# Output weights loaded two rows per partition and reordered on chip, w_down seven rows per partition, new order tables

## The chip, the cores and the metric

The kernel runs on one core of a Trainium2 chip, which has eight. The core has five engines that run side by side, each with its own instruction stream: TensorE (PE; its weight loads are shown as PEld), VectorE (DVE), ScalarE (ACT), GpSimd (POOL) and SyncE (SP), which here issues every DMA. Sixteen DMA engines move data between the chip's memory (HBM) and the on-chip memory (SBUF). TensorE writes its results to a second on-chip memory, PSUM. The metric is the device time of one launch in microseconds (us); smaller is better.

## The reference

One decode step for four sequences through two layers. Each layer is an attention block and a gated feed-forward block, both with a residual; both layers use the same weights and the same caches.

```python
# attention: B=4, D=512, 32 query heads in 8 groups of 4, Sk=4096, Dh=128
q = layernorm(x) @ wq                     # wq [512, 4096]
p = softmax(q @ k_cache.T * 128**-0.5)    # per head, over 4096 keys
x = x + (p @ v_cache) @ wo                # wo [4096, 512]
# feed-forward: F=1792
h = sigmoid(n @ w_gate) * (n @ w_up)      # n = layernorm(x)
x = x + h @ w_down                        # w_down [1792, 512]
```

The caches are bf16: for every sequence b (0 to 3) and every key/value group u (0 to 7) there is one K block and one V block of 4096 x 128, 1.049 MB each (1024 KB). That makes 64 blocks, all of them needed in both layers.

## The kernel before

**Units and steps.** A unit is one (layer, b, u); there are 64. Two units with neighbouring u form a pair, and the main loop runs over 33 steps: step g computes the scores and the softmax of pair g and the values (P times V) of pair g-1. `ORDER` fixes which pair each step has; the two layers are interleaved. In this text K8 or V8 is the block of unit 8, which is the first unit of pair 4.

**Slots.** K and V blocks land in 12 slots of 1 MB. The four megabytes of wq become four more slots when wq has been used for the last time (`wq_done`). A table `RET` says which blocks stay in their slot from layer 0 to layer 1 and are not loaded again: 31 of 128. So the DMA stream is 97 block loads plus wq, wo, w_gate, w_up and w_down, 115.6 MB.

**The stream.** All loads stand in one list, written as strings in `LOADS` (k: next K block, v: next V block, o: next eighth of wo, s: next half of w_gate, w_up or w_down). `pump()` issues from the head of that list on SP as long as a slot is free, and stops at the first block that finds none. Slots come free in program order: after `scores` of a unit (its K slot) and after `pv` of a unit (its V slot), unless the block stays. SP issues in order, so one load that waits for a slot holds up everything behind it.

**A step.** On PE: `scores` (32 matmuls for a pair, two groups of 16, the first of which may be issued early, at the place `FIRST_AT[g]` of the step before), `spread_max`, `pv` of the previous pair (two groups of 32), `ptrans` (two transposes of the exponentials), `sums`, and now and then a `wo` pair (32 matmuls). On DVE: `k_turn` (the 32x32 transpose of a K block, whole or in two halves), the maximum, and small work. On ACT: the exponential and the 16 copies that put `ptrans` in place, of which `SHARE[g]` groups of four go to DVE. `STEP[g]` codes three choices: modulo 3, where the first `k_turn` stands; the next bit, whether the first `pv` stands ahead of `spread_max`; the last bit, whether the second `k_turn` is cut in halves around the softmax. A place inside a step is numbered 0 to 8.

**Passes.** When the last pair of a sequence's layer-0 attention is done, 23 small stages carry x through the output product, the layer norm, w_gate and w_up (`wide`, 56 matmuls each), the gate, w_down (`down`, 56 matmuls), the second layer norm and the new queries. They are serial, and `PLACES[b]` lays them out over the places of about two steps; (1, 8) is place 8 of the step that closes the sequence, (2, 0) place 0 of the next. The four passes begin at 83.0, 142.3, 196.5 and 253.8 us of the span, for sequences 0, 1, 2 and 3. After the last step a tail does the same for all four sequences at once, in layer 1.

**Layouts that the change touches.** `wparts` gives the source and the destination of every weight load. Before, an eighth of wo (four heads, 512 rows) is loaded with row p of head h in partition p, so each piece in memory is one row, 1 KB. The two halves of w_down hold two consecutive rows per partition, 2 KB pieces; therefore `wide_mm` picks w_gate and w_up columns with a step of 2, so that the result falls into the order in which w_down lies.

Of the kernel before, what the change touches and what calls it, by code (L numbers as in the profile page):

```python
# [55 lines left out]

PLACES = [
    (
        (2, 1), (2, 2), (2, 2), (2, 2), (2, 2), (2, 2),
        (2, 2), (2, 2), (2, 3), (2, 3), (2, 3), (2, 3),  # L60
        (2, 3), (2, 3), (2, 3), (2, 3), (2, 5), (2, 8),
        (3, 1), (3, 5), (3, 5), (3, 6), (3, 6),
    ),
    (
        (1, 8), (2, 0), (2, 0), (2, 0), (2, 0), (2, 2),
        (2, 2), (2, 2), (2, 2), (2, 4), (2, 5), (2, 5),
        (2, 7), (3, 1), (3, 1), (3, 1), (3, 2), (3, 2),
        (3, 2), (3, 5), (3, 5), (3, 6), (3, 6),
    ),
    (  # L70
        (1, 8), (1, 8), (1, 8), (1, 8), (1, 8), (1, 8),
        (1, 8), (2, 0), (2, 2), (2, 3), (2, 3), (2, 4),
        (2, 5), (2, 8), (2, 8), (3, 0), (3, 0), (3, 0),
        (3, 0), (3, 1), (3, 2), (3, 5), (3, 5),
    ),
    (
        (1, 8), (1, 8), (1, 8), (1, 8), (1, 8), (1, 8),
        (1, 8), (2, 0), (2, 2), (2, 3), (2, 3), (2, 4),
        (2, 5), (2, 7), (2, 8), (3, 0), (3, 0), (3, 0),
        (3, 0), (3, 1), (3, 2), (3, 5), (3, 5),  # L80
    ),
]


FIRST_AT = (
    1, 2, 8, 2, 2, 1, 8, 2,
    7, 2, 4, 3, 3, 4, 8, 8,
    1, 8, 4, 2, 2, 2, 8, 2,
    5, 1, 2, 7, 2, 2, 2,
)  # L90

LOADS = (
    "oosk", "vvkok", "", "vkkkvvok", "okokkv", "vskkovoksssskkvvkvvvkkvk", "", "",
    "kkvvkkvvk", "", "", "vvkkvv", "", "kvkk", "", "",
    "vkvkvkvkvkkkk", "vvvvvkkvvk", "vk", "", "kvkkvvkvkvvkvkvkkv", "", "", "",
    "", "vvkkvkvkv", "vkk", "", "", "vvkkv", "", "kkvkvvv",
    "kvvkkvvvv",
)


SHARE = (
    0, 0, 0, 2, 0, 1, 0, 0,
    0, 0, 1, 0, 0, 1, 0, 0,
    1, 0, 0, 1, 0, 0, 0, 2,
    1, 0, 1, 2, 1, 0, 1,
)


WO_AT = (
    3, 2, 1, 0, 2, 1, 3, 2,  # L110
    0, 3, 2, 0, 0, 3, 2, 1,
    0, 2, 0, 0, 1, 0, 1, 2,
    1, 2, 1, 2, 0, 0, 0, 0,
)


# [5 lines left out]
)  # L122


STEP = (
    9, 7, 10, 1, 0, 0, 7, 1,
    1, 6, 6, 7, 9, 8, 0, 6,
    6, 3, 6, 6, 6, 6, 6, 6,
    9, 6, 6, 7, 1, 6, 6, 6,
    7,  # L130
)


# [101 lines left out]
def bass_interleave_layers__gqa_block_cached__glu_gated_glu__decode_kernel(  # L235
# [17 lines left out]
    P = 128  # L253
# [128 lines left out]
    for kinds in LOADS:  # L382
        for kind in kinds:
            if kind == "o":
                loads.append(("wo", got["o"]))
            elif kind == "s":
                loads.append(w_small.pop(0))
                continue
            else:
                need(kind, got[kind])  # L390
            got[kind] += 1
# [3 lines left out]

    KH = KF // 2
    wparts = {
        "wo": lambda n: (wo_sb[:, n * REP:(n + 1) * REP, :],
                         A_wo[n * REP * P:(n + 1) * REP * P, :].rearrange("(h p) n -> p h n", p=P)),
        "wg": lambda n: (wg_sb[:, 2 * n:2 * n + 2, :].rearrange("p i f -> p (i f)"),  # L400
                         B_w_gate[2 * n * P:(2 * n + 2) * P, :].rearrange("(p i) f -> p (i f)", i=2)),
        "wu": lambda n: (wu_sb[:, 2 * n:2 * n + 2, :].rearrange("p i f -> p (i f)"),
                         B_w_up[2 * n * P:(2 * n + 2) * P, :].rearrange("(p i) f -> p (i f)", i=2)),
        "wd": lambda n: (wd_sb[:, 8 * n:min(KF, 8 * n + 8), :].rearrange("p (j i) n -> p j (i n)", i=2),
                         B_w_down[8 * n * P:min(KF, 8 * n + 8) * P, :].rearrange("(j p i) n -> p j (i n)", p=P, i=2)),
    }
    assert KF == 2 * KH
    wkeys = {"wg": ["wg0", "wg1"], "wu": ["wu0", "wu1"], "wd": ["wd0", "wd1"]}
# [52 lines left out]
    def dve(fn, reads=(), writes=()):  # L461
        return S.inst("dve", fn, reads=reads, writes=writes)
# [52 lines left out]
    for p in range(2):  # L515
        dve((lambda p: lambda e: e.memset(qz_sb[p][:, :, :], 0.0))(p), writes=[f"qz{p}"])
    dve(lambda e: e.memset(M_ps[1][:, :], 0.0), writes=["M1"])

    def head_masks():
        dve(  # L520
            lambda e: e.tensor_reduce(half_f, ident_bf.rearrange("p (s w) -> p w s", s=4), AX.X, ALU.add),
            reads=IDENT,
            writes=QC,
        )
        dve(
            lambda e: e.tensor_reduce(
                head_s.rearrange("p (u h) -> p u h", u=2),
                half_f.rearrange("p (u a h) -> p u h a", u=2, h=REP),
                AX.X,
                ALU.add,  # L530
            ),
            writes=QC,
        )
        dve(lambda e: e.tensor_copy(head_b[:, :], head_s), reads=QC, writes=["head"])
        for u in range(2):
            dve(
                (lambda u: lambda e: e.tensor_copy(
                    mask_f[:, :, u, :, :],
                    head_b[:, u * REP:(u + 1) * REP].unsqueeze(1).unsqueeze(1).broadcast_to([P, 4, 4, REP]),
                ))(u),  # L540
                reads=["head"],
                writes=[f"mask{u}"],
            )
        dve(
            lambda e: e.tensor_reduce(half_f, ident_bf.rearrange("p (n h) -> p n h", h=REP), AX.X, ALU.add),
            reads=IDENT,
            writes=QC,
        )
        dve(
            lambda e: e.tensor_reduce(  # L550
                strip_f.rearrange("p (s a) -> p s a", s=4),
                half_f.rearrange("p (s u a) -> p s a u", s=4, u=2),
                AX.X,
                ALU.add,
            ),
            writes=QC,
        )
        dve(lambda e: e.tensor_copy(strip_b[:, :], strip_f), reads=QC, writes=["strip"])
        dve(lambda e: e.memset(rowk_f, -exp_scale), writes=["rowk"])
        dve(lambda e: e.memset(zero_f, 0.0), writes=["rowk"])  # L560
        dve(
            lambda e: e.tensor_reduce(blk_f, ident_bf.rearrange("p (a c) -> p a c", a=4), AX.X, ALU.add),
            reads=IDENT,
            writes=["blk"],
        )
# [176 lines left out]
    def wide_mm(nb, which, f0, f1, M, mk):  # L742
        wsb, keys = ((wg_sb, wkeys["wg"]), (wu_sb, wkeys["wu"]))[which]
        fns = []
        for fc in range(f0, f1):
            for k in range(KD):
                fns.append(
                    (lambda fc, k: lambda e: e.matmul(  # L748
                        M[:, 64 + fc * nb:64 + (fc + 1) * nb],
                        lhsT=wsb[:, k, bass.ds(2 * P * (fc // 2) + fc % 2, P, step=2)],  # L750
                        rhs=xc_bf[:, k, 0:nb],
                        start=(k == 0),
                        stop=(k == KD - 1),
                    ))(fc, k)
                )
        S.group("pe", fns, reads=["xcb"] + keys, writes=[mk])
# [388 lines left out]
    def oplace(l, b):  # L1145
        o = owner.get((l, b), (l, b))
        return {(0, 0): 0, (0, 1): 1, (0, 2): 0, (0, 3): 1, (1, 3): 0}[o], 1 if (l, b) in partner else 0
# [16 lines left out]

    def wo_mm(g, p):
        l, b, u = seq[2 * g]
        n, _ = oplace(l, b)
        pb = partner[l, b][1] if (l, b) in partner else None
        nb = 1 if pb is None else 2
        for c, lb in enumerate([(l, b)] if pb is None else [partner[l, b], (l, b)]):  # L1170
            assert held.pop((n, u, c)) == lb
        fns = []
        for c in range(KD):
            for r in range(2 * REP):
                fns.append(
                    (lambda c, r: lambda e: e.matmul(  # L1176
                        O_ps[p][:, 64 + 2 * c:64 + 2 * c + nb],
                        lhsT=wo_sb[:, u * REP + r, bass.ds(2 * P * (c // 2) + c % 2, P, step=2)],
                        rhs=oT_sb[n][:, u * REP + r, 0:nb],
                        start=(r == 0),  # L1180
                        stop=(r == 2 * REP - 1),
                    ))(c, r)
                )
        S.group(
            "pe", fns, reads=[f"oT{n}_{u}_{c}" for c in range(nb)] + [f"wo{u}", f"wo{u + 1}"], writes=[f"O{p}"]
        )

    def wo_add(g, p):
# [18 lines left out]
    ln_a(0, Bn)  # L1207
    ln_b(Bn)
    head_masks()
    k_turn(0)  # L1210
    pump()
    k_turn(1)
    pump()
    q_mm(Bn, 0, HQ)
    q_spread(0, Bn)
    q_blocks(0)

# [29 lines left out]
    assert all(a[1] < b[0] for a, b in zip(spans, spans[1:])), spans  # L1247

    def do_steps(g, w):
        for st in steps.pop((g, w), ()):  # L1250
            st()
        new = g + 1 < NP and fresh.get(seq[2 * g + 2][:2]) == g
        if new and w == PLACES[seq[2 * g + 2][1]][-1][1]:
            q_blocks(g + 1)
        if g + 1 < NP and w == (8 if new else FIRST_AT[g]):
            scores(g + 1, 0)
            pump()
# [134 lines left out]
                close(sg, k)  # L1392
        do_steps(k, 8)
    assert not waiting
    assert not steps
    assert not loads and len(free) == NSLOT + KD

    def x_rows():
# [115 lines left out]
```

## Time and profile before

| what | value |
|---|---|
| median of 3 runs | 314.08 us (311.87 to 314.35) |
| the profiled execution | 313.99 us; its span in the profile is 312.2 us |
| HBM read | 115.61 MB, 370 GB/s over the span |
| DMA busy share of the span (main queue) | 92.5% |
| PE / DVE / ACT / POOL busy | 69% / 59% / 39% / 8% |
| transfers of wo, 8 of 512 KB | 13.5 us from issue to landing (median) |
| transfers of w_down | 1024 KB and 768 KB |
| last V piece landed | 298.4 us |
| last DVE instruction before the store | 309.68 us |

How to read it: the program's first instruction is at 0. Besides the totals, the profile cuts the span into 40 slices of 7.8 us and gives, for each slice, the busy tenths of every engine, the busy share of the 16 DMA engines and the GB/s that they moved. A second view gives the same sums for any window. The timeline lists the instructions of an engine in order, equal ones merged, with the idle time ahead of them and what ended it in brackets. A transfer's landing time is its issue time plus the time from issue to landing in the view of its source line.

### The profile page before, as it was taken

Reading aid. Unit: us, or ns where it says so; the run is one execution under the profiler, and the core shown is the slowest. Engines: PE = TensorE matmul, PEld = TensorE weight load, DVE = VectorE, ACT = ScalarE, POOL = GpSimd, SP = SyncE. Lnnn points to the kernel's source line nnn. Section 1 sums busy time; section 2 is a strip of 40 time slices with the busy share of each in tenths; the row PEclk is TensorE's granted clock in tenths of the full one; section 3 lists DMA queues with packets and bytes.
Section 4 is the critical chain, followed back from the end, with each engine's and each line's share of the span. In section 5 each row is a group of like instructions: output and inputs, shape, how many; then the busy total and the mean of one; then the engine's idle time right before and its main releaser. Section 6 shows DMA issues by size and latency. Waiting matters only on the chain. (4 is left out here: it accounts for less than half of the span.)

```text
span 312.2 us, 12077 instructions
## 1 busy us (share of the span) xinstructions
PE 215.0 (69%) x5204; PEld 157.6 (50%) x5204; DVE 185.2 (59%) x528; ACT 120.3 (39%) x521; POOL 25.9 (8%) x106
## 2 busy tenths in 40 slices
PE   1320447453578876869997958899776668888896
PEld 0310226232365554648665745675555466365686
DVE  4413585575435348485645979674994657358623
ACT  0000254430410576544445645434762351446610
POOL 0000000000000100110010011001011000020200
PEclk9999999999999995555555555555565555565555
DMA  7999999999997999999999999999999976999900
GB/s 291 400 419 408 421 412 394 417 416 399 408 401 302 420 423 421 414 418 400 362 366 407 422 420 408 407 355 411 418 420 418 419 326 225 359 379 421 367 16 3
DMA packets 21217, 116.39 MB, mean 373 GB/s; under 512 B 1960, under 2 KB 6060, under 8 KB 8492
## 3 DMA queue, kind: packets, MB, share of 16 engines
q1 hardware_dynamic: 21164, 115.62, 92.5%
q8 instruction: 41, 0.67, 0.9%
q14 instruction: 12, 0.10, 0.1%
HBM read 115.61 MB, written 0.00 MB: 370 GB/s over the span
## 5 line engine op out<-in xcount | busy, mean ns | idle before, releaser
L1081 ACT ACTIVATE pT<-PT 32x64 bf16<-32x64 f32 x436 | 93.9, 215 | 63.9 <-PE PT L1056 53.9
L925 DVE STREAM_TRANSPOSE slot<-slot 128x1024 f32<-128x1024 f32 (+1 forms) x57 | 98.4, 1730 | 25.9 <-DMA slot<-in_A_k_cache_dram 25.8
L940 PE MATMUL S_ps<-slot,qz 128*32 128x256 bf16 x976 | 61.6, 408 | 23.2 <-DVE slot L925 13.3
L1098 PE MATMUL O_ps<-pT,slot 128*128 128x4 bf16 x1952 | 60.6, 166 | 16.4 <-DMA slot<-in_A_v_cache_dram 10.0
L1098 PEld LDWEIGHTS O_ps<-pT,slot 128*128 128x128 bf16 x1952 | 56.7, 104 | 21.5 <-DMA slot<-in_A_v_cache_dram 10.1
L940 PEld LDWEIGHTS S_ps<-slot,qz 128*32 128x32 bf16 x976 | 28.6, 127 | 38.1 <-DVE slot L925 14.3
L1011 ACT ACTIVATE pe<-S_ps,small 128x256 bf16<-128x256 f32 x32 | 15.5, 485 | 66.2 <-DVE small L999 34.8
L1025 POOL TENSOR_TENSOR small<-small 128x1 f32<-128x1 f32 x64 | 12.4, 194 | 232.8 <-ACT pe L1011 230.3
L1176 PE MATMUL O_ps<-oT,wo 128*128 128x2 bf16 (+1 forms) x640 | 20.0, 165 | 3.7 <-issue 3.2
L1158 DVE TENSOR_TENSOR oT<-O_ps,rden 128x8 bf16<-128x8 f32 x32 | 5.2, 164 | 29.1 <-PE O_ps L1098 26.2
L1176 PEld LDWEIGHTS O_ps<-oT,wo 128*128 128x128 bf16 x640 | 18.8, 104 | 4.8 <-issue 3.2
L963 DVE TENSOR_REDUCE small<-S_ps 128x1 f32<-128x256 f32 x32 | 13.2, 411 | 11.8 <-PE S_ps L940 11.6
L1056 PE MATMUL PT<-ident_bf,pe 128*128 128x128 bf16 x64 | 11.9, 288 | 7.2 <-ACT pe L1011 7.1
L818 PE MATMUL M_ps<-wq,xc_bf 128*1 128x512 bf16 x128 | 15.7, 608 | 0.3
L732 POOL TENSOR_TENSOR qz<-qc,small 128x128 bf16<-128x128 bf16 x32 | 12.6, 401 | 39.2 <-ACT qc L718 39.2
L1075 DVE CAST pT<-PT 32x64 bf16<-32x64 f32 x60 | 13.2, 220 | 2.8 <-PE PT L1056 0.7
L718 ACT ACT_TABLE_LOAD x1 | 1.3, 1283 | 32.6 <-PE M_ps L707 32.6
L707 PE MATMUL M_ps<-qT,ident_bf 128*32 128x32 bf16 (+1 forms) x80 | 1.8, 213 | 15.9 <-DVE qT L689 14.7
L986 PEld LDWEIGHTS MS<-row_max,mask_f 128*128 128x128 bf16 x64 | 4.1, 107 | 15.7 <-DVE row_max L969 12.7
L986 PE MATMUL MS<-row_max,mask_f 128*128 128x16 bf16 x64 | 6.9, 182 | 7.0 <-DVE row_max L969 6.9
L999 DVE CUSTOM_DVE_ANT_0 junk<-MS,small 128x16 bf16<-128x16 f32 x32 | 6.8, 213 | 7.8 <-PE MS L986 7.4
L1034 PEld LDWEIGHTS MS<-head_b,small 128*128 128x128 bf16 x96 | 5.0, 107 | 12.4 <-issue 11.1
(94 smaller groups left out, 190.1 us busy)
## 6 DMA issues: line engine op xcount, KB each, us to landing
slot<-in_A_v_cache_dram SPq DMA_DIRECT2D x49, 1024.0 KB, 10.7
slot<-in_A_k_cache_dram SPq DMA_DIRECT2D x42, 1024.0 KB, 11.5
wq<-in_A_wq_dram SPq DMA_DIRECT2D x4, 1024.0 KB, 8.0
wo<-in_A_wo_dram SPq DMA_DIRECT2D x8, 512.0 KB, 13.5
wq<-in_A_k_cache_dram SPq DMA_DIRECT2D x3, 1024.0 KB, 12.0
slot<-in_A_v_cache_dram SPq DMA_DIRECT2D x8, 256.0 KB, 17.4
wg<-in_B_w_gate_dram SPq DMA_DIRECT2D x2, 896.0 KB, 15.8
wu<-in_B_w_up_dram SPq DMA_DIRECT2D x2, 896.0 KB, 13.6
```

The costliest lines, as they stand in the source:

```text
L732: lambda e: e.tensor_tensor(qz_sb[z][:, :, 0:4 * REP].rearrange("p i (a r) -> p i a r", r=REP), qc_sb[:, b, u:u + 2, :, :].rearrange("p u ...
L818: (lambda k, st: lambda e: e.matmul(M_ps[h][32 * st:32 * st + 1, :], lhsT=xc_bf[:, k, 0:1], rhs=wv[:, k, h, :, st, :], start=(k == 0), sto ...
L925: dve(lambda e: e.transpose(kf, kf), writes=[f"s{st}"])
L940: (lambda t, b2, e_, w0, s: lambda e: e.matmul(S_ps[p][32 * s:32 * s + 8 * REP, 0:2 * P], lhsT=qzf[:, w0:w0 + 8 * REP], rhs=ktv[:, :, s, : ...
L963: lambda e: e.tensor_reduce(m, S_ps[p][:, 0:2 * P], AX.X, ALU.max),
L1011: lambda e: e.activation(to, frm, ACTF.Exp, bias=nm_sb[p], scale=exp_scale, accum_out=sm_sb[p][0],),
L1025: (lambda n: lambda e: e.tensor_tensor(sm_sb[p][n + 1], sm_sb[p][n], top(sm_sb[p][n]), ALU.subtract))(n),
L1056: (lambda j: lambda e: e.matmul(PT[:, j * P:(j + 1) * P], lhsT=pe_sb[p][:, j, :], rhs=ident_bf[:, :], start=True, stop=True))(j)
L1075: (lambda dst, frm: lambda e: e.tensor_copy(dst, frm))(dst, frm),
L1081: (lambda dst, frm: lambda e: e.activation(dst, frm, ACTF.Copy))(dst, frm),
L1098: (lambda x, c, j: lambda e: e.matmul(O_ps[p][:, ul * REP:(ul + 1) * REP], lhsT=vv[:, x * JG + c * 2 + j, :], rhs=pT[:, x, j, 2 * c + ul, ...
L1176: (lambda c, r: lambda e: e.matmul(O_ps[p][:, 64 + 2 * c:64 + 2 * c + nb], lhsT=wo_sb[:, u * REP + r, bass.ds(2 * P * (c // 2) + c % 2, P, ...
```

## The change

Three things.

1. **wo.** Each eighth of wo is loaded with two consecutive rows per partition (2 KB pieces). Rows 2p and 2p+1 of a 256-row block then sit in partition p, which is not the order that the head-wise product wants. TensorE therefore reorders it: `wo_spread` builds two 0/1 matrices of 128 x 128 in `row_sb`, and `wo_turn(m, ...)` takes one block of 256 rows (m = 0 to 15): for each half of the 64 partitions two matmuls of 64 rows x 512 columns into a PSUM bank, then one ACT copy and one DVE copy of 128 x 512 back over the block. `WO_TURN` gives the place of each turn: four ahead of the first step, twelve between place 0 of step 0 and place 1 of step 4.
2. **w_down.** Each half is 7 consecutive rows per partition (7 KB pieces, two equal loads of 896 KB). `wide_mm` therefore takes its weight columns with a step of 7 instead of 2.
3. **Tables.** `PLACES`, `FIRST_AT`, `LOADS`, `SHARE`, `WO_AT` and `STEP` are all new; `ORDER` and `RET` are not. `WO_ORDER` loads the eighths of wo as 2, 3, 0, 1, 4 to 7, all of them among the first 13 weight and block loads after wq. At the start, the query product `q_mm` is issued before the first two `k_turn` instead of after them.

```diff
 PLACES: of sequence 1, the second tuple, and of sequence 3, the last
-        (1, 8), (2, 0), (2, 0), (2, 0), (2, 0), (2, 2),
-        (2, 2), (2, 2), (2, 2), (2, 4), (2, 5), (2, 5),
-        (2, 7), (3, 1), (3, 1), (3, 1), (3, 2), (3, 2),
-        (3, 2), (3, 5), (3, 5), (3, 6), (3, 6),
+        (1, 8), (2, 0), (2, 0), (2, 1), (2, 1), (2, 1),
+        (2, 2), (2, 2), (2, 2), (2, 5), (2, 5), (2, 5),
+        (2, 6), (3, 0), (3, 1), (3, 1), (3, 1), (3, 1),
         (3, 2), (3, 5), (3, 5), (3, 6), (3, 6),
...
-        (1, 8), (1, 8), (1, 8), (1, 8), (1, 8), (1, 8),
-        (1, 8), (2, 0), (2, 2), (2, 3), (2, 3), (2, 4),
-        (2, 5), (2, 7), (2, 8), (3, 0), (3, 0), (3, 0),
-        (3, 0), (3, 1), (3, 2), (3, 5), (3, 5),
+        (1, 8), (2, 0), (2, 0), (2, 0), (2, 0), (2, 1),
+        (2, 1), (2, 2), (2, 2), (2, 3), (2, 5), (2, 5),
+        (2, 8), (3, 0), (3, 0), (3, 0), (3, 1), (3, 1),
+        (3, 2), (3, 2), (3, 2), (3, 5), (3, 5),
...
 FIRST_AT = (
-    1, 2, 8, 2, 2, 1, 8, 2,
-    7, 2, 4, 3, 3, 4, 8, 8,
-    1, 8, 4, 2, 2, 2, 8, 2,
-    5, 1, 2, 7, 2, 2, 2,
+    8, 2, 5, 6, 3, 2, 3, 4,
+    8, 2, 8, 7, 2, 4, 8, 7,
+    8, 4, 1, 2, 5, 7, 8, 2,
+    1, 4, 2, 7, 8, 7, 2,
 LOADS = (
-    "oosk", "vvkok", "", "vkkkvvok", "okokkv", "vskkovoksssskkvvkvvvkkvk", "", "",
+    "oooko", "kookoks", "osvkkkkvv", "kv", "kvvskvkvk", "sssvkvvkvvvkkvk", "", "kkvk",
...
+WO_ORDER = (2, 3, 0, 1, 4, 5, 6, 7)
+WO_TURN = (
+    (-1, 0), (-1, 0), (-1, 0), (-1, 0),
+    (3, 1), (1, 8), (0, 0), (0, 2),
+    (0, 6), (0, 7), (2, 4), (0, 3),
+    (0, 2), (1, 2), (4, 1), (3, 5),
+)
 STEP = (
-    9, 7, 10, 1, 0, 0, 7, 1,
-    1, 6, 6, 7, 9, 8, 0, 6,
-    6, 3, 6, 6, 6, 6, 6, 6,
-    9, 6, 6, 7, 1, 6, 6, 6,
-    7,
+    5, 6, 3, 4, 3, 0, 2, 4,
+    7, 6, 11, 10, 9, 0, 9, 7,
+    6, 9, 6, 6, 0, 9, 9, 0,
+    7, 3, 6, 8, 9, 11, 6, 9,
+    0,
...
-        "wo": lambda n: (wo_sb[:, n * REP:(n + 1) * REP, :],
-                         A_wo[n * REP * P:(n + 1) * REP * P, :].rearrange("(h p) n -> p h n", p=P)),
+        "wo": lambda n: (wo_sb[:, n * REP:(n + 1) * REP, :].rearrange("p (a i) n -> p a (i n)", i=2),
+                         A_wo[n * REP * P:(n + 1) * REP * P, :].rearrange("(a p i) n -> p a (i n)", p=P, i=2)),
...
-        "wd": lambda n: (wd_sb[:, 8 * n:min(KF, 8 * n + 8), :].rearrange("p (j i) n -> p j (i n)", i=2),
-                         B_w_down[8 * n * P:min(KF, 8 * n + 8) * P, :].rearrange("(j p i) n -> p j (i n)", p=P, i=2)),
+        "wd": lambda n: (wd_sb[:, n * KH:(n + 1) * KH, :].rearrange("p i n -> p (i n)"),
+                         B_w_down[n * KH * P:(n + 1) * KH * P, :].rearrange("(p i) n -> p (i n)", p=P)),
...
+    def wo_spread():
+        dve(lambda e: e.memset(row_sb[:, 0:2 * P], 0.0), writes=["row0"])
+        for i in range(2):
+            for h in range(2):
+                rows = slice(64 * h, 64 * h + 64)
+                dve(
+                    (lambda i, rows: lambda e: e.tensor_copy(spread_w[i][rows, i:P:2], ident_bf[rows, rows]))(i, rows),
...
+    def wo_turn(m, ps, key):
+        n, a = WO_ORDER[m // 2], m % 2
+        c = n * REP + 2 * a
+        for h in range(2):
+            rows = slice(64 * h, 64 * h + 64)
...
+                    (lambda h, i, rows: lambda e: e.matmul(
+                        ps[h][:, :],
+                        lhsT=spread_w[i][rows, :],
+                        rhs=wo_sb[rows, c + i, :],
+                        start=(i == 0),
+                        stop=(i == 1),
...
+            lambda e: e.activation(wo_sb[:, c, :], ps[0][:, :], ACTF.Copy),
...
+            lambda e: e.tensor_copy(wo_sb[:, c + 1, :], ps[1][:, :]),
...
-                        lhsT=wsb[:, k, bass.ds(2 * P * (fc // 2) + fc % 2, P, step=2)],
+                        lhsT=wsb[:, k, bass.ds(KH * P * (fc // KH) + fc % KH, P, step=KH)],
...
     head_masks()
+    wo_spread()
+    q_mm(Bn, 0, HQ)
+    for m in wo_steps.pop((-1, 0), ()):
+        wo_turn(m, (M_ps, S_ps)[m % 2], "MS"[m % 2])
     k_turn(0)
     pump()
     k_turn(1)
     pump()
-    q_mm(Bn, 0, HQ)
     q_spread(0, Bn)
```

From step 6 on, the new `LOADS` differ from the old ones by a few swaps of neighbours and moves of one or two places; the byte position of each block that the prediction names is given there.

## The prediction

> **What bounds the kernel now.** I read the slices first, for the DMA rate over time.
>
> ```profile
> GB/s 291 400 419 408 421 412 394 417 416 399 408 401 302 420 423 421 414 418 400 362 366 407 422 420 408 407 355 411 418 420 418 419 326 225 359 379 421 367 16 3
> ```
>
> The stream runs at about 420 GB/s nearly everywhere, and ends in slice 38 of 40. It is the bound, except where it sags. Then the same sums in windows around the sags, beside a calm one (after the window: us, busy us and counts of PE, PEld, DVE, ACT, POOL, granted clock, DMA share, GB/s):
>
> ```profile
> 60.00:64.00 4.00, 1.85 (x55) 1.30 (x48) 3.04 (x5) 2.60 (x13) 0.00 (x0) 1.00 1.02 420
> 98.00:101.00 3.00, 2.72 (x67) 1.66 (x64) 2.48 (x4) 0.00 (x0) 0.00 (x0) 1.00 0.54 145
> 145.00:168.00 23.00, 21.23 (x513) 15.25 (x511) 12.85 (x48) 8.97 (x37) 2.28 (x9) 0.50 0.98 370
> 204.00:220.00 16.00, 15.50 (x346) 10.21 (x346) 10.00 (x36) 7.27 (x31) 1.52 (x6) 0.50 0.98 384
> 255.00:262.00 7.00, 6.75 (x179) 5.50 (x179) 6.02 (x18) 1.72 (x8) 0.00 (x0) 0.50 0.40 125
> 262.00:278.00 16.00, 13.44 (x288) 8.61 (x292) 7.81 (x36) 6.14 (x26) 1.50 (x6) 0.61 0.97 361
> ```
>
> A window loses (421 - its rate) / 421 of its length: 2.0 (call it hole A), 2.8 (B), 1.4 (C), 4.9 and 2.3 us (together D), 13.4 us in all. In B, C and D PE is busy over 84% of the time: there a pass runs on PE beside the steps, slots come free late, and the stream starves. The timeline of PE shows D:
>
> ```profile
> 251.15 1.01 PE L1098 MATMUL O_ps<-pT,slot 128*128 128x4 bf16 x32 [1.79 <-DMA slot<-in_A_v_cache_dram]
> ...
> 255.60 1.85 PE L748 MATMUL M_ps<-xc_bf,wg 128*128 128x1 bf16 x56
> 257.32 0.89 PE L748 MATMUL M_ps<-xc_bf,wu 128*128 128x1 bf16 x28
> 258.13 1.04 PE L940 MATMUL S_ps<-slot,qz 128*32 128x256 bf16 x16
> ...
> 266.26 1.01 PE L1098 MATMUL O_ps<-pT,slot 128*128 128x4 bf16 x32 [2.05 <-DMA slot<-in_A_v_cache_dram]
> ```
>
> The pass of sequence 3 starts when V49 lands (251.1). Its `wide` matmuls stand ahead of the scores at 258.13, whose end frees the slot of V51; SP issues V51 at 259.27, it lands 6.9 us later, and the PE waits 2.05 us for it in the middle of the pass. So the time is a relay: the stream up to V9, V21, V35, V49 (each closes a sequence), then a pass at PE's pace, four last steps from 279 to 297, and a tail that no DMA feeds.
>
> **Part 1, piece size: -1.45 us.** Landing minus previous landing, summed over the eight wo transfers, is 11.45 us for 4.19 MB: 366 GB/s. The last V pieces also go in 2 KB: seven of 0.262 MB land from 293.93 to 298.44, 407 GB/s. At that rate wo takes 10.3 us, 1.15 less. The two w_down transfers (2 KB) took 4.67 us; at the 421 of large pieces 4.36, so 0.3 less. Bounds: 0, and 1.5 + 0.3 if wo came at full rate. The Trainium skill has a smaller price ("DMA: Bandwidth & Descriptors", section "Why small descriptors are slow (HBM only)"): about 3 cycles per packet of 32-byte beats, by which wo would gain some 4%, 0.5 us, an estimate; the rows differ by 11%.
>
> **Part 2, the turns: hidden, 0.** Sixteen times two copies of 128 x 512 from PSUM: by the same size in the passes
>
> ```profile
> L838 DVE TENSOR_SCALAR row<-M_ps,newt 128x512 bf16<-128x512 f32 x4 | 3.0, 750 | 8.8 <-PE MS L986 4.9 <-PE M_ps L848 3.8
> L831 ACT ACTIVATE row<-M_ps,newt 128x512 bf16<-128x512 f32 x4 | 2.7, 687 | 1.7 <-PE M_ps L818 1.7
> ```
>
> that is 12 us of DVE and 11 of ACT. PE: 64 matmuls of 512 columns, which no row shows at full width. L818 does eight of one row in 1.02 us, 0.13 each; four of those may run side by side, so 0.13 to 0.51 us each, 8 to 33 us; I take the upper. All of it lies between 17 and about 75 us, where the stream, not compute, sets the pace. Cover, in the worst place: by byte position (13.5 us after wq, 1.29 per wo eighth, 2.375 per MB) the new list brings V1 at 53, V3 at 60.6, V5 at 68, V7 at 80; the slots they free are wanted 5 us later or more (closest is the slot that V7 itself takes: free at 70, wanted at 75.5). Turns in step 0 also wait for wo's seventh eighth (30 us); step 0's exponential stood at 39.7 before and may be as late as 47, where step 1 waits for K5 anyway. If that cover fails, every us late at V7 is a us of stream. Four turns and the small copies of `wo_spread` (0.2 us each) lie ahead of the first `k_turn`, while K0 is still on its way.
>
> **Part 3, w_down and hole A: -1.0 us.** The pass of sequence 0 waited for w_down:
>
> ```profile
> 92.61 1.85 PE L867 MATMUL M_ps<-qT,wd 128*128 128x1 bf16 x56 [1.80 <-DMA wd<-in_B_w_down_dram]
> ```
>
> It ends at 35.9 MB of the list in both. V8, though, moves from 38.0 to 37.0 MB, ahead of K13; V9 stays at 39.1. Before, V8 landed at 97.44, freed a slot, V10 went out at 98.74 and needed 4.8 us from an empty queue; V11 followed V9 (99.85) at 101.0. Now V8 lands at about 93.5, V10 goes out at 94.8, well ahead of V9's landing at 98.4; V11 goes out at 99.5 and lands at 104.5, where a full queue would give 103.4. About 1 us of hole is left of 2. So V13 lands 2.45 us earlier, and so does V21, since the eleven blocks between them take 27.4 us at 2.49 with no hole.
>
> **Part 4, the tables from V21 on: -0.3 us.** *Pass of sequence 1 (B): +1.2.* `FIRST_AT[11]` goes from 3 to 7: sixteen score matmuls (1.05 us) that filled a wait of 2.0 us at 137.3 now stand between the last `pv` and the start of the pass, on a PE that has no gap of note until 162. `FIRST_AT[12]` puts another group ahead of `spread_max`. Between 0 and 2. *Pass 2 (C): 0*, one `wide` half (0.9 us) moves behind scores(19,1); between -1 and +1. *Pass 3 (D): -1.5.* Only `ln_a` now stands ahead of scores(26,1), and `STEP[25]` no longer holds the exponential for K53. Those scores can run at 254.4 instead of 258.1, V51 goes out at about 255.5, in time to land at 261.1 behind V50, and the 2.05 us wait goes; 0.25 to 0.5 us is paid where the scores stand ahead of the norm. What is late next is PE itself: with the row durations, the second norm's matmul comes at 266.7 instead of 267.3, the queries' eight groups at 267.3 instead of 268.9, `wq_done` at 271.3 instead of 272.9. Bounds: 0, and -4 if the whole stream gain counted. *Last four steps and tail: 0.* No DMA wait is in them now; `SHARE` takes 4 to 8 copies of 0.215 us off ACT, late scores give some back; within 1 either way.
>
> **Sum.** -1.45 - 1.0 + 1.2 - 1.5 = -2.75, from 313.99 us (span 312.2 and 1.8 around it; the median, 314.08, is the same): **311.2 us**. The step of 7 is taken at no cost: a step of 2 has none.
>
> ```profile
> L748 PE MATMUL M_ps<-xc_bf,wu x224: 165/165/187, 88.9 to 259.9; 128*128 128x1 bf16 x112
> L1098 PEld LDWEIGHTS O_ps<-pT,slot 128*128 128x128 bf16 x1952 | 56.7, 104 | 21.5 <-DMA slot<-in_A_v_cache_dram 10.1 <-ACT pT L1081 6.4 <-issue 4.8
> L748 PEld LDWEIGHTS M_ps<-xc_bf,wu 128*128 128x128 bf16 x224 | 6.6, 104 | 0.3
> ```
>
> Both loads, contiguous and with step 2, take 104 ns and repeat every 31 to 33 ns.
>
> **Rivals.** *R1, the tables do more:* scores(12,0) falls into a wait after all (B 0), C gains 1, and D's whole hole closes because the stream, not PE, ruled the end (-4): 313.99 - 1.45 - 1.0 - 1 - 4 = 306.5. For it: D lost 7.2 us. Against: PE is 84 to 97% busy there. *R2, the gain is given back:* B +2, C +1, D -0.5: 314. For it: the same PE share. *R3, slower: the weight read with step 7.* 14 bytes lie between neighbours. Upper end: a load repeats every 66 ns, twice today's (the slowest weight loads in the profile, f32, take 317 ns against 104). Then 112 `wide` matmuls cost 3.7 us more in each of the three gap-free passes and 3.1 in the tail (1.57 + 1.49 of span today), 14.2 in all: 325. It decides from 6 ns per load (2.75 us over 448 loads) and is slower by 1% from 13 ns (5.85 us). For it: no row has a step over 2 at this place. Against: step 2 costs nothing at all. The Trainium skill states a rule for this ("Advanced Engine Details and Errata", section "SBUF Cachelines"): full speed needs two hits on each 16-byte line, which a 14-byte step mostly misses. Another page of the Trainium skill ("SBUF — State Buffer", section "Door 1: The DMA port swizzle") counts a step of up to 8 bf16 as free. The trace, with steps 1 and 2 alone, agrees with both. *R4:* the turns eat their cover and the stream starves before V9, 3 us or more: 317 or more; against it stand the 5 us above. That the change does not do what it says: the transfers' sizes and the pieces are plain in the code; I give it nothing.
>
> **How the numbers follow.** Forecast 0.46, with its own range 309 to 313.5; R1 0.22; R2 0.16; R3 0.12; R4 0.04. About 1%, 3.1 us, is what a measurement of this kernel can tell from no change; the bounds are 310.9 and 317.2. Of the forecast some 0.17 lies below 310.9, with R1: faster 0.39. The rest of it, 0.29, and R2 less its tail beyond 317 (0.03): same 0.42. R3, R4 and that tail: slower 0.19. The range: below 306 lies a third of R1 (0.07), above 320 some two thirds of R3, which runs from 317 to 325, and a part of R4 (0.10), together under 0.2: 306 to 320.
>
> **What would show it.** Packets of 2 KB for wo at over 400 GB/s; the step-0 exponential anywhere before 47; no hole at V10, a small one at V11; V21 near 137.2; scores(26,1) ahead of the `wide` matmuls and no 2 us wait in pass 3; `wide` groups of 56 in 1.85 us as before. A `wide` group over 2.5 us makes R3; a DMA hole before V9 makes R4; a B window that loses more than now makes R2.

## The result, and the profile after

The changed kernel is slower: median 321.94 us (321.2 to 326.11), against 312.89 us (311.13 to 314.35) for the kernel before; the ratio is 1.0285, 95% interval 1.0239 to 1.0332, some 9 us. The ratios here and below are taken from fast runs, without a slow one such as that of 326.11 us. Its profiled execution took 321.78 us, with a span of 320.0. The forecast was 311.2 us, the range ended at 320. What happened is the mechanism of R3, the weight read with step 7, which had a chance of 0.12.

The slices of the changed kernel, GB/s over 40 slices of 8.0 us:

```profile
GB/s 289 410 408 415 414 419 423 418 419 422 417 348 309 384 416 424 419 393 297 308 358 399 418 424 418 412 343 373 350 425 417 421 377 129 397 413 418 301 4 1
```

The stream still runs at about 420 between the sags, but the sags at the first three passes (slices 12 to 14, 19 to 21, 27 to 29) are wider, and the one of the last pass reaches 129 (slice 34; before, 225). The same windows as before the change (us, then busy us and counts of PE, PEld, DVE, ACT, POOL, granted clock, DMA share, GB/s):

```profile
98.00:101.00 3.00, 2.93 (x50) 1.08 (x42) 2.67 (x9) 0.20 (x1) 0.00 (x0) 0.50 0.84 303
145.00:168.00 23.00, 22.40 (x464) 16.95 (x460) 13.59 (x51) 6.44 (x26) 1.53 (x6) 0.50 0.85 323
204.00:220.00 16.00, 15.74 (x294) 10.66 (x293) 9.46 (x34) 3.23 (x12) 0.39 (x2) 0.50 0.96 360
255.00:262.00 7.00, 5.82 (x120) 4.29 (x118) 3.61 (x12) 3.88 (x18) 0.73 (x3) 0.50 0.95 394
262.00:278.00 16.00, 15.74 (x303) 11.73 (x301) 9.52 (x32) 5.08 (x21) 0.38 (x2) 0.50 0.69 254
```

In 145 to 168 PE is busier (22.4 us against 21.2) and yet does less: 464 matmuls instead of 513. So a matmul takes longer on average. The timeline of PE shows which, in the last pass (start, us, engine, line, operation, count):

```profile
261.62 3.33 PE L804 MATMUL M_ps<-xc_bf,wg 128*128 128x1 bf16 x56
264.80 3.35 PE L804 MATMUL M_ps<-xc_bf,wu 128*128 128x1 bf16 x56
268.08 1.05 PE L996 MATMUL S_ps<-slot,qz 128*32 128x256 bf16 x16
...
269.13 0.89 PE L923 MATMUL M_ps<-qT,wd 128*128 128x1 bf16 x28
...
309.18 0.59 PE L804 MATMUL M_ps<-xc_bf,wg 128*128 128x4 bf16 x8
...
312.60 3.12 PE L804 MATMUL S_ps<-xc_bf,wu 128*128 128x4 bf16 x56
315.65 1.69 PE L1489 MATMUL PT<-wd,slot 128*32 128x128 bf16 x56
```

A `wide` group of 56 takes 3.33 us instead of 1.85, so a load comes every 59 ns on average instead of every 33; the `down` matmuls on the same PE keep their pace (0.89 for 28). From the first `wide` matmul of the tail to the product with w_down it takes 6.47 us. The same place in the kernel before, 3.69 us:

```profile
304.17 0.37 PE L748 MATMUL M_ps<-xc_bf,wg 128*128 128x4 bf16 x8
...
307.86 1.69 PE L1427 MATMUL PT<-wd,slot 128*32 128x128 bf16 x56
```

The view of the line has the single loads (min/median/max ns):

```profile
L804 PEld LDWEIGHTS M_ps<-xc_bf,wu x224: 130/152/154, 89.4 to 267.9; 128*128 128x128 bf16 x112
L804 PE MATMUL M_ps<-xc_bf,wu x224: 191/192/213, 89.4 to 268.0; 128*128 128x1 bf16 x112
```

The load went from 104 to 152 ns, and the starts stand 53 ns apart, not 27 (medians inside a group; the means above also hold the one or two gaps of some 250 to 300 ns that most groups have). It is 53 ns in the tail too, where the stream has ended (2 GB/s from 304 us on), so the other traffic of that moment is not the reason.

### The profile page after: what moved, and what is told of

The parts are those of the page before. It is cut to its first block, busy times and chain, and to the rows that moved or that the text cites. A ratio compares the mean times of both kernels' runs of the same rounds, so it can differ in the third digit from the quotient of the medians.

```text
span 320.0 us, 12235 instructions
## 1 busy us (share of the span) xinstructions
PE 245.8 (77%) x5268; PEld 176.2 (55%) x5268; DVE 203.5 (64%) x583; ACT 121.5 (38%) x501; POOL 25.8 (8%) x106
## 4 chain that ended last, share of the span: by engine, by line
PE 42%; DMA 32%; DVE 10%; SPq 9%; issue 4%; ACT 2%; DVEq 0%; ACTq 0%
DMA slot<-in_A_v_cache_dram 32%; PE M_ps L804 9%; PE O_ps L1154 9%; PE S_ps L996 7%; PE M_ps L874 5%; DVE slot L981 4%; SPq L447 4%; SPq L466 4%; PE O_ps L1233 3%; PE M_ps L923 2%; DVE pT L1131 2%; PE M_ps L635 1%; PE M_ps L701 1%; ACT pT L1137 1%; PE PT L1112 1%
## 5 line engine op out<-in xcount | busy, mean ns | idle before, releaser
L1137 ACT ACTIVATE pT<-PT 32x64 bf16<-32x64 f32 x400 | 85.7, 214 | 51.1 <-PE PT L1112 41.9
L981 DVE STREAM_TRANSPOSE slot<-slot 128x2048 f32<-128x2048 f32 (+1 forms) x55 | 97.9, 1784 | 4.9 <-DMA slot<-in_A_k_cache_dram 4.7
L1154 PE MATMUL O_ps<-pT,slot 128*128 128x4 bf16 x1952 | 62.5, 166 | 26.1 <-DMA slot<-in_A_v_cache_dram 18.1
L996 PEld LDWEIGHTS S_ps<-slot,qz 128*32 128x32 bf16 x976 | 29.1, 128 | 26.8 <-DVE slot L981 9.9
L1131 DVE CAST pT<-PT 32x64 bf16<-32x64 f32 x96 | 21.2, 221 | 4.3 <-PE PT L1112 1.3
L561 ACT ACTIVATE wo<-M_ps 128x512 bf16<-128x512 f32 x14 | 8.3, 596 | 31.2 <-PE M_ps L551 31.0
L551 PE MATMUL M_ps<-wo,row 64*128 64x512 bf16 x56 | 14.4, 610 | 6.5 <-DVE wo L566 4.3
L804 PEld LDWEIGHTS M_ps<-xc_bf,wg 128*128 128x128 bf16 x280 | 16.5, 154 | 0.7 <-DVE xc L648 0.2
L804 PE MATMUL M_ps<-xc_bf,wg 128*128 128x1 bf16 (+1 forms) x280 | 16.3, 192 | 0.2
L566 DVE CAST wo<-M_ps 128x512 bf16<-128x512 f32 x14 | 9.5, 677 | 8.6 <-PE M_ps L551 8.6
L804 PE MATMUL M_ps<-xc_bf,wu 128*128 128x1 bf16 x224 | 13.1, 192 | 0.2
## 6 DMA issues: line engine op xcount, KB each, us to landing
slot<-in_A_k_cache_dram SPq DMA_DIRECT2D x42, 1024.0 KB, 10.3
wq<-in_A_k_cache_dram SPq DMA_DIRECT2D x3, 1024.0 KB, 11.7
wg<-in_B_w_gate_dram SPq DMA_DIRECT2D x2, 896.0 KB, 17.8
```

The lines of the kernel that those rows point to most:

```text
L551: (lambda h, i, rows: lambda e: e.matmul(ps[h][:, :], lhsT=spread_w[i][rows, :], rhs=wo_sb[rows, c + i, :], start=(i == 0), stop=(i == 1), ...
L804: (lambda fc, k: lambda e: e.matmul(M[:, 64 + fc * nb:64 + (fc + 1) * nb], lhsT=wsb[:, k, bass.ds(KH * P * (fc // KH) + fc % KH, P, step=KH)],
L981: dve(lambda e: e.transpose(kf, kf), writes=[f"s{st}"])
L996: (lambda t, b2, e_, w0, s: lambda e: e.matmul(S_ps[p][32 * s:32 * s + 8 * REP, 0:2 * P], lhsT=qzf[:, w0:w0 + 8 * REP], rhs=ktv[:, :, s, : ...
L1131: (lambda dst, frm: lambda e: e.tensor_copy(dst, frm))(dst, frm),
L1137: (lambda dst, frm: lambda e: e.activation(dst, frm, ACTF.Copy))(dst, frm),
```

## The experiments

They come in three groups: what part of the change costs, what the step costs, and where it reaches the end of the run. Where two versions of the kernel are compared across groups, their ratios to the kernel before are used, or their medians (the kernel before had 312.66, 312.67 and 312.64 in the three).

**e1_after_wd2: the change with w_down as it was.**

```diff
-        "wd": lambda n: (wd_sb[:, n * KH:(n + 1) * KH, :].rearrange("p i n -> p (i n)"), ...
+        "wd": lambda n: (wd_sb[:, 8 * n:min(KF, 8 * n + 8), :].rearrange("p (j i) n -> p j (i n)", i=2), ...
...
-    lhsT=wsb[:, k, bass.ds(KH * P * (fc // KH) + fc % KH, P, step=KH)],
+    lhsT=wsb[:, k, bass.ds(2 * P * (fc // 2) + fc % 2, P, step=2)],
```

> The changed kernel with w_down back at two rows per partition and the wide weight columns back at a step of 2; wo, the turns and all new tables stay. Theory T (the weight read with step 7 is the loss): a wide group of 56 goes from 3.33 us back to 1.85, 1.5 us twice in each of four passes and 3.2 us in the tail, so 12 us off if pass 0 is covered and 15 if not: 307 to 310 us, ratio to the kernel before about 0.985. Rival U (the turns and the early wo loads cost the time) and rival V (the new order tables cost it): no more than 1 us off, 320 to 322 us.

Measured: 311.6 us (309.78 to 312.77), ratio 0.9975 (0.9947 to 1.0003). The whole loss is gone: 10.3 us of the changed kernel's time by the medians, 9.7 by the ratios, come from these two lines. That is less than the 12 to 15 us expected. The new tables and the turns together cost nothing that can be measured.

**e2_before_wd7: the kernel before, with these two lines alone.** The edit is the reverse of the one above, on the old kernel.

> The kernel before with w_down alone changed to seven rows per partition, step 7 in the wide weight columns, old tables and old wo. T: +3.0 us in each of the three passes that PE bounds and +3.2 in the tail, +12, and up to 3 more if pass 0 counts: 325 to 328 us. U and V: the same as before within 1 us, 312 to 314.

Measured: 324.59 us (322.01 to 325.89), ratio 1.0379 (1.0314 to 1.0444), 11.9 us, no less than in the changed kernel and a little below the 325 to 328 expected. So the loss doesn't need the new tables.

**e3_tables_only: the tables without the turns.** wo in 1 KB pieces and w_down as before, `wo_spread` and `wo_turn` not issued.

```diff
-    for m, kw in enumerate(WO_TURN):
-        wo_steps.setdefault(kw, []).append(m)
...
-    wo_spread()
```

> The changed kernel with both layouts undone: wo in 1 KB pieces without any turn, w_down with two rows per partition and step 2. What stays is the new tables and the earlier query product. Against e1 this leaves out the turns and pays 1.15 us for the small wo pieces. If the turns are hidden: 1 us slower than e1, 308 to 311. U: faster than e1 by several us. V: 318 or more.

Measured: 313.29 us (311.24 to 316.86), ratio 0.9997 (0.996 to 1.0033). The tables alone are worth nothing that can be measured, and the 308 to 311 us expected were missed, as e1 was above its own. E1 less e3, the wo layout with its turns, is -1.7 us by the medians and -0.7 by the ratios, and the two intervals overlap: that the turns are hidden fits, but the time does not prove it.

**e9_read2: the changed kernel with 7 KB pieces of w_down, but step 2 in the loads.** This separates the two lines of e1.

```diff
-    lhsT=wsb[:, k, bass.ds(KH * P * (fc // KH) + fc % KH, P, step=KH)],
+    lhsT=wsb[:, k, bass.ds(2 * P * (fc // 2) + fc % 2, P, step=2)],
```

> The changed kernel with w_down in pieces of 7 KB as it has it, but the wide weight loads at step 2. The columns then don't match the order of w_down, so each feed-forward block multiplies wrong rows, with the same amount of work. Theory (the loss is the weight loads alone): the wide groups take 1.85 us again and the time is that of e1_after_wd2, 311 to 312, at most 0.3 us less for the larger pieces. Rival (the layout of w_down itself costs, in its transfer or in the products that read it): a part of the 10.3 us stays, 313 or more.

Measured: 311.15 us (309.89 to 312.28), ratio 0.9966 (0.9933 to 0.9999). This run differs from the changed kernel in that one line, and 10.8 us are gone. The layout of w_down costs nothing that can be measured, nor does its transfer; the loads do. The line's view in this run:

```profile
L804 PEld LDWEIGHTS M_ps<-xc_bf,wu x224: 104/104/116, 88.2 to 260.2; 128*128 128x128 bf16 x112
```

**e4_steps: what a step costs.** The kernel before, with another step in each `wide` group; other columns are multiplied, so other numbers are computed, with the same amount of work.

```diff
+    STEPS = ([4, 4, 3, 3, 5, 5, 7, 7, 1, 12], [7, 7, 4, 4, 6, 6, 8, 8, 2, 2])
...
-    lhsT=wsb[:, k, bass.ds(2 * P * (fc // 2) + fc % 2, P, step=2)],
+    lhsT=wsb[:, k, bass.ds(start(fc), P, step=step)],
```

> The kernel before, with the wide matmuls taking other columns (so the numbers it computes are others): gate groups with steps 4, 3, 5, 7 in passes 0 to 3, up groups with 7, 4, 6, 8, the tail with 1, 12 and 2. Read from the trace alone: the time of a group of 56 by step. If a step of up to 8 bf16 is free, steps 3 to 8 take 1.85 us and only the change of w_down's landing could explain the loss, so T falls. If two hits per 16-byte line are needed, steps 3 and 4 take 1.85 us, 5 to 8 about 3.3. If the read slows with the bytes between columns, the time grows from step 3 on. Pass 0 lies at the full granted clock, the later ones at half of it: step 7 in pass 0 against pass 3 tells whether that clock matters.

Its one time is 321.2 us. The timeline of PE, its `wide` groups alone; their steps are, in order, 4, 7, 3, 4, 5, 6, 7, 8, 12, 2 (a second half with step 6, one with step 8 and a group of 8 with step 1 are left out):

```profile
87.29 2.21 PE L755 MATMUL M_ps<-xc_bf,wg 128*128 128x1 bf16 x56
89.36 3.35 PE L755 MATMUL M_ps<-xc_bf,wu 128*128 128x1 bf16 x56
...
147.01 1.92 PE L755 MATMUL M_ps<-xc_bf,wg 128*128 128x1 bf16 x56
149.65 2.21 PE L755 MATMUL M_ps<-xc_bf,wu 128*128 128x1 bf16 x56
...
201.33 2.58 PE L755 MATMUL M_ps<-xc_bf,wg 128*128 128x1 bf16 x56
203.77 1.46 PE L755 MATMUL M_ps<-xc_bf,wu 128*128 128x1 bf16 x28
...
259.75 3.33 PE L755 MATMUL M_ps<-xc_bf,wg 128*128 128x1 bf16 x56
262.95 1.84 PE L755 MATMUL M_ps<-xc_bf,wu 128*128 128x1 bf16 x28
...
310.69 2.97 PE L755 MATMUL M_ps<-xc_bf,wg 128*128 128x4 bf16 x48
313.51 1.63 PE L755 MATMUL S_ps<-xc_bf,wu 128*128 128x4 bf16 x56
```

Median distance from one load to the next, inside a group:

| step | 1, 2 | 3 | 4 | 5 | 6 | 7 | 8 | 12 |
|---|---|---|---|---|---|---|---|---|
| ns | 27 | 28 | 33 | 40 | 47 | 53 | 60 | 58 |
| 16-byte lines that 128 columns touch | 16, 32 | 48 | 64 | 80 | 96 | 112 | 128 | 128 |

From step 4 to step 8 the distance grows by 6.75 ns per step, and step 12, which reaches over half as much again, costs no more than step 8. So it is not the distance between neighbours that is paid for. The number of 16-byte lines (the size in the rule that the prediction quotes) fits every row: 27 ns as a floor, and 0.47 to 0.52 ns for each line once they are 64 or more. Of the three patterns that the expectation names none fits as it stands: a step of 8 is not free, steps 5 to 8 are not alike, and the cost stops growing at step 8. One run shows this, with one to two groups per step, and step 12 stands in the tail alone.

**e7_tail7: step 7 in the tail alone.** e1 with a list of steps: 7 for the `wide` groups of the tail, 2 for all others.

```diff
+    STEPS = ([2, 2, 2, 2, 2, 2, 2, 2, 7, 7], [2, 2, 2, 2, 2, 2, 2, 2, 7, 7])
```

> The kernel of e1_after_wd2 (all of the change, but w_down in two rows per partition), with the step of 7 in the two wide groups of the tail alone; the ten other wide groups keep step 2. It leaves out the match between the columns and the order of w_down in the tail, so the last feed-forward block multiplies the right number of wrong rows: the amount of work is the same. Theory (each load pays for the 16-byte lines it touches, and in the tail nothing covers it): the two tail groups take 6.3 us of span instead of 3.1, the time is e1's plus 3.2 us, 314.8, and the stream's last V piece lands where e1 has it, near 297.0. Rival 1 (the tail waits for something else beside the loads): less than 1 us above e1, 312.5 or less. Rival 2 (the loss is not the weight loads but the pieces of w_down): e1's time, 311.6.

Measured: 315.1 us (313.17 to 316.15), ratio 1.009 (1.0051 to 1.0129), 3.5 us above e1. The last V piece lands at 296.5 as in e1 (297.0). The timeline of PE at the end:

```profile
301.40 0.59 PE L813 MATMUL M_ps<-xc_bf,wg 128*128 128x4 bf16 x8
...
304.82 3.13 PE L813 MATMUL S_ps<-xc_bf,wu 128*128 128x4 bf16 x56
307.88 1.69 PE L1498 MATMUL PT<-wd,slot 128*32 128x128 bf16 x56
```

6.48 us from the first load to the product, as in the changed kernel; 2.8 us more than before, and the time is longer by as much, within its error. Nothing covers the tail.

**e10_pass123_7: step 7 in the passes of sequences 1, 2 and 3.**

```diff
+    STEPS = ([2, 2, 7, 7, 7, 7, 7, 7, 2, 2], [2, 2, 7, 7, 7, 7, 7, 7, 2, 2])
```

> The kernel of e1_after_wd2 with the step of 7 in the wide groups of the passes of sequences 1, 2 and 3, and step 2 in the first pass and the tail. In those passes it multiplies wrong rows, with the same amount of work. Theory 1 (the three places add up): of the 10.3 us the tail has 3.5 (e7_tail7 less e1_after_wd2, median 315.1 - 311.6) and the first pass 1.8 (ratio 1.0032 less 0.9975), so 5.0 are left: 316.6, with the last V piece some 5 us later than in e1_after_wd2, at 302. Theory 2 (every us on TensorE counts in the three gap-free passes, 3.0 us each, as the prediction's R3 had it with the measured group): 9.0, so 320.6. Rival (a late first pass makes the later ones dear): under 3 us, 314.5 or less.

Measured: 318.28 us (318.14 to 319.08), ratio 1.0189 (1.0127 to 1.0252), 6.4 us above the same kernel without it in the same group of runs (311.93), 7.3 by the ratios. That lies between the two theories: of the 9.0 us that three passes lose on PE, seven to eight tenths reach the end. By the landings, V21 to V49 takes 116.6 us (112.4 in e1, 112.1 in e11), so the passes of sequences 1 and 2 cost some 4.3 us of their 6.0; V49 to the last V piece takes 47.5 against 44.5, the full 3.0; and after the last piece 0.9 to 1.9 us come back. A likely reason is that the end of the stream is not all that the last steps wait for; no run tests it. This run and the changed kernel agree at V49: both land it at 256.9.

**e8_pass0_7: step 7 in the first pass alone.**

```diff
+    STEPS = ([7, 7, 2, 2, 2, 2, 2, 2, 2, 2], [7, 7, 2, 2, 2, 2, 2, 2, 2, 2])
```

> The kernel of e1_after_wd2 with the step of 7 in the two wide groups of the first pass (sequence 0, 83 to 101 us) alone; all other wide groups keep step 2. In that pass it multiplies wrong rows, with the same amount of work. Theory (a slower pass costs time only as far as it delays a slot that the stream waits for): the groups take 3.33 instead of 1.85 us, and of these 3.0 us about 1 reaches V9, as in the changed kernel, where V9 lands 1.0 us later than in e1; V13 1.0 to 1.3 us later; the time 0.5 to 1.3 us above e1's 311.6, so 312.1 to 312.9. Rival 1 (every us on TensorE counts, as the prediction's R3 priced it): 314.6. Rival 2 (later holes take it back, as in the stretch from V13 to V21): within 0.3 of e1.

Measured: 313.76 us (310.95 to 315.73), ratio 1.0032 (0.9994 to 1.0071). That is 1.8 us above e1 by the ratios, between the theory (up to 1.3) and rival 1 (3.0), with an error as large. Its trace has V9 0.4 us later than e1, V13 1.8. But the three places together, 3.5 + 6.4 + 1.8 = 11.7, are more than the 10.3 of the whole (each is known to about 1 us), and the changed kernel and e10, one with and one without step 7 in the first pass, both land V21 at 140.3. What the first pass costs stays open between 0 and 1.8 us.

**e6_pass3_old: e1 with the places of the last pass as they were.** The last tuple of `PLACES` is that of the kernel before.

> The kernel of e1_after_wd2 with the places of the last pass (sequence 3) as they were before the change; everything computed. Theory (the prediction's step D: scores(26,1) ahead of the wide groups free V51's slot 2 to 4 us earlier and the 2.05 us wait in the pass goes): the stretch from V49 to the last V piece is again 47 us instead of 44.4, the time 1.5 to 2.9 us above e1's 311.6, so 313.1 to 314.5. Rival 1 (the gain of that stretch comes from STEP and FIRST_AT, not from the places): within 0.5 of e1, 311.1 to 312.1. Rival 2 (the place of the stages is worth nothing because the stream has slack later): the V51 wait is back, the last V piece lands as in e1.

Measured: 312.41 us (310.99 to 315.0), ratio 1.0017 (0.998 to 1.0053): 0.8 us above e1 by medians, 1.3 by ratios, below what was expected. In the trace V51 goes out at 261.6, not 256.9, and V49 to the last V piece takes 45.8 us: 1.4 more than e1's 44.4, 1.5 less than the 47.3 of before. V51 lands at 266.3, just as PE comes to it, so the 2 us wait does not come back. By one trace of each, the places are half of what this stretch gained; which of the other tables brought the rest is open.

**e5_first11: e1 with `FIRST_AT[11]` and `[12]` as they were.**

```diff
-    8, 2, 8, 7, 2, 4, 8, 7,
+    8, 2, 8, 3, 3, 4, 8, 7,
```

> The kernel of e1_after_wd2 with FIRST_AT[11] set back from 7 to 3 and FIRST_AT[12] from 2 to 3, as before the change; everything computed. Theory (the prediction's step B: sixteen score matmuls of 1.05 us that filled a wait now stand in the gap-free pass): V21 to K33 0.8 to 1.2 us shorter than in e1, the time 0.8 to 1.2 us below e1's 311.6, so 310.4 to 310.8, a version below both kernels. Rival 1 (the later scores pay elsewhere: slots free later, a hole moves): within 0.3 of e1. Rival 2 (the early scores take the place of work that the stretch ahead of V21 needs): 0.5 to 1 above e1.

Measured: 311.76 us (310.34 to 313.53), ratio 0.9998 (0.9968 to 1.0029). Rival 1 holds: no gain. V21 to K33 takes 28.3 us, inside the 28.0 to 29.1 of six traces that have the new entries and step 2 in this pass (e1, e6, e7, e8, e9, e11). The early scores do fill the wait again, and the pass starts 0.8 us earlier after V21; by the second norm 0.4 of that are left.

**e11_after_wd2_again: e1 once more.**

> The kernel of e1_after_wd2 once more, as the base beside e9_read2 and e10_pass123_7 on the same chip. The ratio to the kernel before should be 0.9975 again, between 0.994 and 1.001: the rest of the change, without the step of 7, is worth 0 to 2 us, and not the 2.75 us of the prediction. If the prediction's sum holds for it, the ratio is 0.991.

Measured: 311.93 us (309.66 to 314.37), ratio 0.9957 (0.9919 to 0.9995). By the two ratios the change without its step of 7 is 0.8 to 1.3 us faster than the kernel before. The interval of e1 includes no change and that of e11 ends just short of it; no kernel here is shown to be 1% faster than the one before.

## Why the prediction was wrong

**The step that failed is "The step of 7 is taken at no cost: a step of 2 has none."** What the runs showed in its place: a load every 59 ns instead of every 33, and 9.7 to 10.8 us more of the whole. Steps 1 and 2 both lie on the floor, where 16 or 32 lines are touched; two points on a floor say nothing of where it ends, and it ends at step 4. The inference from them should have been a bound from both sides, as the other unknown costs had, with a chance near one half. R3 had the mechanism and the sign: it named the place, the 112 matmuls in each gap-free pass and the tail, and a `wide` group over 2.5 us as its mark (measured: 3.33). It was decided from 6 ns per load; measured were 26. Its upper end, 66 ns and 14.2 us, was too high: a load came every 59 ns, a pass lost 3.0 us and not 3.7, and of the 9.0 us in three passes some 6.4 reached the end; the tail lost the 3.1 us forecast (2.8 in the trace, 3.5 in the time).

The Trainium skill's rule quoted there ("Advanced Engine Details and Errata", section "SBUF Cachelines"), that an access needs two hits on each 16-byte line, is borne out in the main: step 4 has two columns per line and costs 33 ns against 27, a little above the floor, and the steps above it rise to 60 ns. The other page of the Trainium skill quoted there, "SBUF — State Buffer", section "Door 1: The DMA port swizzle", by which a step of up to 8 bf16 is free, is contradicted for these loads by the 60 ns at step 8. Between two rules that differ on the very size in question, the trace of before could not decide, and that should have stood in the chances.

**The other steps** can be judged in e1 and e11, where the step of 7 is absent. Their time, 311.6 and 311.9 us, is close to the forecast of 311.2, but partly by luck: the sum was made from an execution of 313.99 us, and the median of the kernel before in the later runs is 312.6. The gain is 0.8 to 1.3 us, not 2.75, and lies between the forecast and R2, in which it is given back. It also comes from elsewhere than forecast: parts 1 and 3, 2.45 us together, had brought nothing by V21, and D brought twice its term.

*Part 1, -1.45:* right as a transfer time. The eight eighths of wo took 10.64 us in the changed kernel and 10.45 in e11 instead of 11.45 (11.78 in e3, which has the new list with 1 KB pieces), and w_down's two halves in the changed kernel 4.37 instead of 4.67: -0.8 to -1.3 and -0.3. wo's rate was 394 GB/s in the changed kernel and 401 in e11, near the 407 of the row that was taken.

*Part 2, hidden:* right. The step-0 exponential stood at 33.8 us in the changed kernel and 33.9 in e11, well before 47. No new hole opened ahead of V9 in e11 and e1 (86 to 98 us: 401 GB/s in e1, 398 before); in the changed kernel that window fell to 366, with the step of 7 in the first pass. The 64 matmuls took some 16.5 us (14.4 for 56), half of the 33 that were allowed. The copies and matmuls on the page of the changed kernel:

```profile
L561 ACT ACTIVATE wo<-M_ps 128x512 bf16<-128x512 f32 x14 | 8.3, 596 | 31.2 <-PE M_ps L551 31.0
L551 PE MATMUL M_ps<-wo,row 64*128 64x512 bf16 x56 | 14.4, 610 | 6.5 <-DVE wo L566 4.3
...
L566 DVE CAST wo<-M_ps 128x512 bf16<-128x512 f32 x14 | 9.5, 677 | 8.6 <-PE M_ps L551 8.6
```

*Part 3, hole A, -1.0:* wrong; nothing was gained. (V9 doesn't close a sequence, as the prediction says: sequence 0 ends with V7, and its pass runs ahead of V9's landing.) A window of the kernel before, then two of e11:

```profile
101.00:112.00 11.00, 9.96 (x212) 6.10 (x210) 4.08 (x18) 7.23 (x31) 1.15 (x4) 1.00 1.01 423
```

```profile
98.00:101.00 3.00, 2.47 (x57) 1.68 (x61) 2.61 (x14) 1.22 (x5) 0.00 (x0) 0.50 0.83 284
101.00:112.00 11.00, 9.75 (x227) 6.12 (x219) 3.98 (x19) 5.93 (x26) 1.88 (x7) 0.50 0.94 365
```

V8 landed at 93.5 as forecast, V9 at 98.5 (98.4), and the hole at 98 to 101 shrank from 2.0 to 1.0 us. A new one opened right behind it: 101 to 112 fell from 423 to 365 GB/s, (421 - 365) / 421 x 11 = 1.5 us. V11 went out 1.4 us earlier than before, but V13, in the forecast 2.45 us earlier, at 104.2, before at 104.7: what frees its slot hardly moved with the stream. By V18 nothing was left (127.1, before 127.2), and V21 landed at 139.5 (e1: 140.2), before at 139.6, forecast 137.2. The prediction followed the slots of V10 and V11 and took the next ones for granted.

*Part 4.* B: V21 to K33 took 28.0 to 29.1 us in six traces, before 27.9; +0.1 to +1.2 where +1.2 was forecast, but e5 shows that `FIRST_AT[11]` and `[12]` are not its cause, or are repaid at once. C: V35 to V49, 57.4 (e11) and 58.1 (e1) against 57.6: 0, as forecast. D: V49 to the last V piece 44.4 us against 47.3, -2.9 where -1.5 was forecast and -4 the bound. The mechanism was right (V51 out at 256 to 257, the 2.05 us wait gone), and the size wrong: PE's own pass was shortened by more than the sum had. Its last large product, the one for the new queries, before:

```profile
268.91 3.92 PE L818 MATMUL M_ps<-wq,xc_bf 128*1 128x512 bf16 x32
```

The same in e1, with the matmuls that begin when V49 has landed:

```profile
252.60 1.02 PE L1154 MATMUL O_ps<-pT,slot 128*128 128x4 bf16 x32 [0.85 <-DMA slot<-in_A_v_cache_dram]
...
267.59 3.83 PE L874 MATMUL M_ps<-wq,xc_bf 128*1 128x512 bf16 x32
```

From V49's landing to this product it took 17.8 us before and 15.0 in e1 and e11: -2.8, forecast -1.6. So the stretch gained what PE gained: PE's pace, and not the stream as R1 had it, fits as what rules it. In e10 this product comes 2.6 us later after V49 than in e1 and the stretch is 3.0 us longer; in e6 it is 0.5 against 1.4, so this is not fully shown. Last steps and tail: 12.8 and 13.8 us behind the last piece, against 13.8: within the 1 us allowed.

## What to carry to other kernels

When a layout change turns a contiguous or paired read of TensorE's weights into a strided one, count the 16-byte lines that each load touches, and multiply by every load that reads that way: here 560 loads (112 in each of four passes and the tail) took 26 ns more each, for 0.3 us saved in the transfers of w_down. Other engines' reads were not tried. A row that shows a small step to be free doesn't cover a larger one; treat it as an unknown with a price on both sides. And when a stream's hole is filled, follow the slots until one is found whose release didn't move, since that is where the hole goes.

## What the runs showed of the hardware

A TensorE weight load of 128 bf16 columns comes every 27 ns up to a step of 2 (28 at step 3), and from step 4 on costs about half a nanosecond per 16-byte line, up to 60 ns when every column has a line of its own (e4_steps). The granted clock made no difference to it between 1.00 and 0.50. Two windows of e4_steps, around a group of step 7 at full granted clock and one at half:

```profile
87.00:93.00 6.00, 5.66 (x116) 5.40 (x116) 1.39 (x9) 0.27 (x1) 0.00 (x0) 1.00 1.05 404
...
259.00:268.00 9.00, 8.64 (x145) 7.89 (x149) 4.71 (x15) 1.58 (x8) 0.00 (x0) 0.50 0.27 86
```

The groups in them took 3.35 and 3.33 us. The changed kernel also has the lower clock earlier in its run (0.50 at 98 to 101 us, before 1.00); the unchanged groups take the same at both (in the kernel before, 16 score matmuls 1.04 us, 64 value matmuls 1.85 us), and two executions of the kernel before at mean granted clocks of 0.584 and 0.869 took 311.42 and 311.27 us. So no part of the 9 us is put down to it.
